# First weights behind the loads of nine units, their scaling queued behind the cast in front, and units 9 to 11 transposed on TensorE

## Chip, cores and metric

The kernel runs on one core of one Trainium2 chip. The metric is the time of one execution on the device, in microseconds (us). Lower is better. Three runs of the kernel before took 585.72, 586.73 and 589.5 us; the median is 586.73.

Engine names as in the profile: PE is TensorE's matmuls, PEld its loads of the stationary operand, DVE is VectorE, ACT is ScalarE, POOL is GpSimd, SP is the engine whose queue issues the transfers (DMAs).

## The reference

Gated linear attention over 4 batches, 8 heads, 768 tokens and a head width of 48, then a two-layer feed-forward network over all 3072 tokens.

```
for t in range(S):
    state = alpha[:, :, t, :, None] * state + np.einsum('bhd,bhe->bhde', k[:, :, t], v[:, :, t])
    y[:, :, t] = np.einsum('bhd,bhde->bhe', q[:, :, t], state)
...
x = np.ascontiguousarray(attn_out.transpose(0, 2, 1, 3)).reshape(B * S, H * D)
h = x @ w_in
g = np.maximum(0.01 * h, h)
out = (g @ w_out).astype(np.float32)
```

q, k, v and alpha are float32. The weights (384 x 2048 and 2048 x 384) are float64, and the kernel reads them as pairs of 32-bit words.

## The kernel before

**Units, blocks, items.** The attention is cut into 24 units: unit u is one chunk of 128 tokens of one batch, the four batches of a chunk one after another (units 0 to 3 have no state yet, line 317). Three units make a block of 384 tokens; there are 8 blocks. The feed-forward network works on a block and one of 16 slices f of 128 hidden columns: one such pair is an item (i, f). A first half (`ffn_in`, line 401) is nine matmuls of 128 x 384 into one of two `ph` banks, then ScalarE (lines 410, 413) and VectorE (411, 415) make the high part gh and the low part gl of the hidden values (three buffers each). A second half (`ffn_out`, line 420) is nine matmuls into the three banks of the block's sums; it is written two items later (LAG). `finish` (434) copies the sums with ScalarE and stores them.

**A unit, step by step.** `scans(u)` transposes alpha, then VectorE makes the running products forward (246) and their reversed counterpart (251). `scaled_q`, `scaled_k` transpose q and k and multiply (266, 274). `scores` are 16 matmuls (283), `mask_scores` copies and masks them, `k_tokens` turns k back, `outputs` makes y and from it x, a high part on ScalarE (342) and a low part on VectorE (343), and `next_state` updates the state. The generator `attention` yields between these steps and overlaps unit u + 1 with unit u. After each third unit, `gather` moves a few rows of x by DMA, and the block's items can start.

**Two ways to transpose** (line 212). Units under EARLY = 9 are loaded with one row per token (`load`, line 113) and transposed on TensorE into PSUM, four transposes per tensor (218). Later units are loaded in another layout by four transfers per tensor (121) and transposed on VectorE by one instruction per tensor (222). The same constant decides in `mask_scores` whether the second half of the scores is masked by ScalarE and GpSimd or by VectorE (291). alpha, q and k have two buffers each, v three; a load of unit u + 2 is written as soon as unit u has been transposed, that of v (`load_values`) for u + 3 in `outputs(u)`.

**Weights.** `load_weights(f)` issues five transfers on SP into one of four raw tiles. `convert(f)` turns float64 into a high and a low float32 part: ScalarE scales the upper words (line 200), VectorE works in six steps (201, 202, 204 to 207), and between them ScalarE casts the high part (203), which line 206 needs.

**PSUM.** Two banks are `ph`. Six belong to two kinds, "a" and "b", three each. At first the attention takes both kinds in turn; from line 457 on only "a", since block 0 keeps its sums in "b", block 1 in "a" and all later blocks in "b".

**What sets the order.** The program is a trace of instructions in the order of the Python code; the tile framework then orders each engine's queue with a timing model of its own (`schedule_with_timeline_sim=True`, line 623), earlier lines first where several are ready. Each engine then works its queue in that order and waits on semaphores. `behind(key)` (line 165) adds an edge: what is written within it, on the engine of the named instruction, is queued behind that instruction. In the kernel before, the attention of units 0 to 5 runs first (lines 446 to 452), with the weight loads of f = 0 to 3 written after its 18th, 26th, 34th and 42nd step. Conversions 0 to 2 stand behind the x of units 3 to 5 on VectorE. Then three items of block 0 are written with the rest of the attention of units 6 to 8 among them (8 steps per item), then three items of block 1, and from f = 3 on pairs: (0, f), (1, f), with the conversion of f + 2. From block 2 on, 1.5 steps of attention are written per item.

Of the kernel before, what the change touches and what calls it, by code (L numbers as in the profile page):

```python
# [9 lines left out]
F32 = mybir.dt.float32  # L10
# [12 lines left out]
def gated_linear_attn_ffn(ctx, tc, q, k, v, alpha, w_in, w_out, out):  # L23
    nc = tc.nc
# [8 lines left out]
    NF = DF // P  # L33
    UPB = 3
    HB = 64
    BR = HB + D
# [3 lines left out]
    NU = len(units)  # L40
# [13 lines left out]
    NBITS, NPW, NRAW = 1, 1, 4  # L54
    T4 = 4
    RUN = T4 * D
    PITCH = RUN + GAP
    EARLY = 3 * UPB
    FIRST = 3
    LAG = 2  # L60
    SL = 8 * UPB


# [34 lines left out]
    def w_out_of(f, n):  # L98
        return w_sb[f][:, n, DM:]

    def loaded(u, i):
        return loads_sb[i][u % len(loads_sb[i])]

# [3 lines left out]
    def load(u, i):  # L107
# [4 lines left out]
        t, src = loaded(u, i), (alpha, q, k)[i]  # L112
        if u < EARLY:
            n = H if u or i else H // 2
# [13 lines left out]
    def load_values(u):  # L128
        if u >= NU:
            return  # L130
        tb, b = units[u]
        nc.sync.dma_start(
            vals_sb[u % NV].rearrange("t (h d) -> t h d", h=H),
            v[b, :, tb * C:(tb + 1) * C, :].rearrange("h t d -> t h d"),
        )
# [24 lines left out]
    runs = [(0, D, 0, 1, 2 * D), (D, GAP, 6 * D, NG, 1), (HB, D, D, 1, 2 * D), (BR, GAP, 7 * D, NG, 1)]  # L160


    jobs, made = {}, {}

    def behind(*key):

        return tc.issue_after(made[key].ins) if key in made else nullcontext()

    def load_weights(f):
        if f >= NF:  # L170
# [11 lines left out]
    def convert(f):  # L182
        if f >= NF:
            return
        raw = jobs.pop(f)
        w_sb[f] = cst.tile([P, 2, 2 * DM], F32R, name=f"w{f}")
        hi, lo = w_sb[f][:, HIGH, :], w_sb[f][:, LOW, :]
        if not f64:
            val = raw[:, :, 0:P].bitcast(F32)
            hi, lo = (t.rearrange("p (g f) -> p g f", f=P) for t in (hi, lo))  # L190
            nc.scalar.copy(hi, val)
            nc.vector.tensor_tensor(lo, val, hi.bitcast(F32), ALU.subtract)
            return
        words = raw.rearrange("p g (f w) -> p (g f) w", w=2)
        top, low = words[:, :, 1], words[:, :, 0]
        bits = cvp.tile([P, 2 * DM], I32, name="bits", bufs=NBITS)
        pw = cvp.tile([P, 2 * DM], I32, name="pw", bufs=NPW)
        val, rest = bits.bitcast(F32), pw.bitcast(F32)

        nc.scalar.mul(top.bitcast(F32), top.bitcast(F32), 2.0 ** -112)  # L200
        nc.vector.tensor_scalar(bits, top, 3, 0x7FFFFFF8, ALU.logical_shift_left, ALU.bitwise_and)
        nc.vector.scalar_tensor_tensor(bits, top, -0x80000000, bits, ALU.bitwise_and, ALU.bitwise_or)
        nc.scalar.copy(hi, val)
        nc.vector.tensor_scalar(pw, bits, -0x800000, None, ALU.bitwise_and)
        nc.vector.scalar_tensor_tensor(rest, low.bitcast(U32), 2.0 ** -52, rest, ALU.mult, ALU.mult)
        nc.vector.tensor_tensor(val, val, hi.bitcast(F32), ALU.subtract)
        made["w", f] = nc.vector.tensor_tensor(lo, rest, val, ALU.add)

    def banks4():
        return bank().rearrange("r (p n) -> r p n", p=NP)  # L210

    def transposed(u, i, name, **kw):

        src = loaded(u, i)
        if u < EARLY:
            ps = banks4()
# [69 lines left out]
    def mask_scores(u):  # L286
        ss = live[u].pop()
        sm = [atp.tile([P, NP, C], F32, name="sm", bufs=3) for _ in (0, 1)]
        for s in (0, 1):
            if s and u >= EARLY:  # L290
                nc.vector.tensor_tensor(sm[s], ss[s], mask.unsqueeze(1).broadcast_to([P, NP, C]), ALU.mult)
                continue
            nc.scalar.copy(sm[s], ss[s])  # L293
            nc.gpsimd.affine_select(  # L294
                out=sm[s], in_=sm[s], compare_op=ALU.is_ge, fill=0.0, base=0, pattern=[[0, NP], [1, C]], channel_multiplier=-1
            )
        masked[u] = sm
# [11 lines left out]
    def outputs(u):  # L309
        tb, b = units[u]  # L310
        i, j = divmod(u, UPB)
        pe, qs, ktok = live[u][:3]
        V, W = vals_sb[u % NV], state[b]
        at = i % 3 * (NG + 1)
        y = banks4()

        if tb:
            for p in range(NP):
                nc.tensor.matmul(
                    y[0:BR, p, :], W[0:BR, p, :], qs[0:BR, p, :], start=p == 0, stop=False, skip_group_check=True  # L320
                )
        for p in range(NP):
            for s, lo, m in ((0, 0, D if tb else HB), (1, HB, D)):
                c = (2 * p + s) * D
                nc.tensor.matmul(  # L325
                    y[lo:lo + m, p, :], V[:, c:c + m], masked[u][s][:, p, :],
                    start=not tb and p == 0, stop=p == NP - 1, skip_group_check=True,
                )
        del masked[u]
        kv = None  # L330
        if tb < NC - 1:
            kv = bank()[:, 0:NP * D].rearrange("d (p e) -> d p e", p=NP)
            for p in range(NP):
                for s, lo in ((0, 0), (1, HB)):
                    h = 2 * p + s
                    nc.tensor.matmul(
                        kv[lo:lo + D, p, :], ktok[:, p, lo:lo + D], V[:, h * D:(h + 1) * D], start=True, stop=True
                    )
        load_values(u + NV)
        live[u] = pe, kv  # L340
        xh, xl = (x_sb[0:BR, at:at + NP, n, j * C:(j + 1) * C] for n in (0, 1))
        nc.scalar.copy(xh, y[0:BR])
        made["x", u] = nc.vector.tensor_tensor(xl, y[0:BR], xh.bitcast(F32), ALU.subtract)

    def next_state(u):
# [25 lines left out]
    ready = set()  # L371

    def attention(first, last):

        for u in range(first - 1, last):
            new, old = u + 1 < last, u >= first
            if new:
                scans(u + 1)
                yield
            if old:  # L380
                scores(u)
                yield
                mask_scores(u)
                yield
                k_tokens(u)
                yield
            if new:
                scaled_q(u + 1)
                yield
                scaled_k(u + 1)  # L390
                yield
            if old:
                outputs(u)
                yield
                next_state(u)
                if u % UPB == UPB - 1:
                    gather(u // UPB)
                    ready.add(u // UPB)
                yield
# [40 lines left out]
            nc.sync.dma_start(out[r:r + P, :], o)  # L440


    LOADS = 18, 26, 34, 42
    st = attention(0, EARLY)
    n = 0
    while 1 not in ready:
        next(st)
        n += 1
        if n == 3:
            load_values(NV - 1)  # L450
        if n in LOADS:
            load_weights(LOADS.index(n))
    for f in range(FIRST):
        with behind("x", UPB + f):
            convert(f)
    loaded_f = len(LOADS)
    kinds[:] = "a"


    items = [(0, f, None, SL / FIRST, "b") for f in range(FIRST)]  # L460
    items += [(1, f, f + FIRST if f < LAG else None, 0, "a") for f in range(FIRST)]
    for f in range(FIRST, NF):
        items += [(0, f, f + LAG, 0, "b"), (1, f, None, 0, "a")]
    items += [(i, f, None, SL / NF, "b") for i in range(2, NB) for f in range(NF)]

    gs = {}
    due, emitted, held = 0.0, 0, 0
    for n in range(len(items) + LAG):
        slices = 0
        if n < len(items):  # L470
            i, f, weights, slices, _ = items[n]
            if f == 0:
                if i == 1:
                    for _ in st:
                        pass
                if i == 2:
                    st, held = attention(EARLY, NU), 8
                while i not in ready:
                    next(st)
                emitted, due = 0, 0.0  # L480
            if loaded_f < NF:
                load_weights(loaded_f)
                loaded_f += 1
            if weights is not None:
                with behind("x", EARLY - 1):
                    convert(weights)
            gs[n] = ffn_in(i, f)
        for half in range(2):
            due += slices / 2
            while emitted < due:  # L490

                with behind(*(("w", NF - 1) if held else ())):
                    next(st, None)
                held = max(held - 1, 0)
                emitted += 1
            if half == 0 and n >= LAG:
                i, f, _, _, tag = items[n - LAG]
                ffn_out(i, f, gs.pop(n - LAG), tag)
# [129 lines left out]
```

## Time and profile before

| what | us |
|---|---|
| median of three runs | 586.73 |
| the profiled execution's own time | 587.34 |
| its span, first to last instruction | 585.6 |
| PE busy / PEld busy | 548.0 / 510.8 |
| DVE busy | 397.7 |
| ACT busy | 234.3 |
| POOL busy | 53.2 |
| ACT waiting at line 200 for a DMA of weights, 13 times | 28.4 |
| mean granted TensorE clock, share of full speed | 0.973 |

The span is 1.7 us shorter than the execution's own time. A row of the profile gives an engine, a line of the kernel, the operation, output and inputs, and a count; in order of time it begins with start and length in us, and brackets at its end give how long the engine was idle before it and what it waited for. Lengths of neighbouring rows overlap a little, since an instruction's end and the next one's start are not the same event: pitch from start to start is what an engine really spends. A stage row gives, for a stretch of time, the busy us of each engine, the clock that TensorE was granted, and what the DMA engines did. Stages here do not have one limit: the start, the pairs of blocks 0 and 1, and the long rest from about 216 us differ, and are read apart.

### The profile page before, as it was taken

What the parts mean: (1) busy time and instruction counts of PE and PEld (TensorE: products, weight loads), DVE (VectorE), ACT (ScalarE), POOL (GpSimd) and SP (SyncE); (2) the same over time, 40 slices, a digit from 0 to 9 for tenths busy, and PEclk for the clock granted to TensorE, in tenths of its full rate; (3) what the DMA queues carried; (4) which work ended last, traced back from release to release, by engine and by line L of the source; (5) the groups of instructions that cost most, each with busy time, mean ns of one, the idle gap of its engine ahead of it and who ended that gap; (6) DMA issues with size and microseconds to landing.
All of it is one profiled execution on the core that took longest, in us unless ns stands there. A gap on an engine that the chain in (4) does not pass through costs nothing. (4 is left out here: it accounts for less than half of the span.)

```text
span 585.6 us, 9944 instructions
## 1 busy us (share of the span) xinstructions
PE 548.0 (94%) x3742; PEld 510.8 (87%) x3742; DVE 397.7 (68%) x726; ACT 234.3 (40%) x486; POOL 53.2 (9%) x108
## 2 busy tenths in 40 slices
PE   6887899798989899999999989999999999999995
PEld 4766799687879888999899989998999999999994
DVE  6879854889889989688837775767848553333331
ACT  3553543454344364443533344344433243334332
POOL 4122112000000001011101101101001000000000
PEclk9899689899989999999999999999999999999998
DMA  9999953444320544224512342222311110001001
GB/s 162 192 194 169 175 129 84 120 109 108 109 54 1 120 135 104 61 63 97 141 26 64 73 120 45 64 50 65 99 25 39 35 42 0 1 21 42 0 1 45
DMA packets 92981, 46.62 MB, mean 80 GB/s; under 512 B 57856, under 2 KB 90112, under 8 KB 92928
## 3 DMA queue, kind: packets, MB, share of 16 engines
q1 hardware_dynamic: 92928, 45.93, 36.6%
q8 instruction: 31, 0.51, 0.4%
q14 instruction: 22, 0.18, 0.1%
HBM read 38.83 MB, written 4.72 MB: 74 GB/s over the span
## 5 line engine op out<-in xcount | busy, mean ns | idle before, releaser
L407 PE MATMUL ph<-large,w 128*128 128x384 f32 x1152 | 231.5, 345 | 13.5 <-DVE t L411 6.7
L407 PEld LDWEIGHTS ph<-large,w 128*128 128x128 f32 x1152 | 202.8, 191 | 22.5 <-DVE t L411 10.5
L428 PE MATMUL b<-w,gh 128*128 128x384 f32 x672 | 170.1, 344 | 0.9 <-ACT t L438 0.6
L411 DVE TENSOR_TENSOR t<-ph,t 128x384 f32<-128x384 f32 x128 | 70.1, 551 | 85.7 <-ACT t L410 85.2
L428 PEld LDWEIGHTS b<-w,gh 128*128 128x128 f32 x672 | 120.1, 190 | 5.3 <-ACT gh L413 1.9
L410 ACT ACTIVATE t<-ph 128x384 f32<-128x384 f32 x128 | 62.3, 489 | 144.8 <-PE ph L407 130.9
L428 PE MATMUL b<-w,gl 128*128 128x384 f32 x336 | 107.7, 340 | 1.6 <-DVE gl L415 1.6
L415 DVE TENSOR_TENSOR gl<-t,gh 128x384 fp32r<-128x384 f32 x128 | 70.8, 557 | 38.4 <-ACT gh L413 38.3
L413 ACT CAST gh<-t 128x384 fp32r<-128x384 f32 x128 | 65.4, 512 | 71.6 <-DVE t L411 69.6
L428 PEld LDWEIGHTS b<-w,gl 128*128 128x128 f32 x336 | 62.4, 189 | 3.2 <-DVE gl L415 2.6
L283 PE MATMUL a<-qs,ks 48*128 48x128 f32 x336 | 37.9, 295 | 2.7 <-DVE qs L266 1.7
L283 PEld LDWEIGHTS a<-qs,ks 48*128 48x128 f32 x336 | 31.2, 195 | 10.3 <-issue 5.9
L358 POOL TENSOR_TENSOR small<-us,pe 48x192 f32<-48x192 f32 x32 | 18.5, 577 | 175.1 <-DVE us L357 173.8
L294 POOL TENSOR_SCALAR_AFFINE_SELECT sm<-sm 128x512 f32<-128x512 f32 x33 | 22.0, 672 | 134.7 <-ACT sm L293 134.3
L257 ACT ACTIVATE e<-pc 128x512 f32<-128x512 f32 x24 | 15.2, 632 | 31.9 <-DVE rc L251 17.9
L200 ACT ACTIVATE raw<-raw 128x768 f32<-128x768 f32 x16 | 14.6, 916 | 28.4 <-DMA raw<-in_moe_w_in_dram 28.4
L246 DVE TENSOR_TENSOR_SCAN pc<-e,small 128x128 f32<-128x128 f32 x60 | 22.0, 422 | 0.5
L325 PE MATMUL a<-sm,small 128*48 128x128 f32 x288 | 22.2, 279 | 0.0
L428 PE MATMUL a<-w,gh 128*128 128x384 f32 x96 | 21.7, 349 | 0.0
L222 DVE STREAM_TRANSPOSE ks<-small 128x512 f32<-128x512 f32 x15 | 16.6, 1104 | 6.9 <-PE a L304 6.9
L258 POOL COPY pe<-pc 128x4 f32<-128x4 f32 x24 | 7.9, 328 | 144.7 <-DVE pc L246 144.2
L222 DVE STREAM_TRANSPOSE e<-small 128x512 f32<-128x512 f32 x15 | 16.6, 1104 | 6.0 <-ACT e L257 5.8
(77 smaller groups left out, 537.2 us busy)
## 6 DMA issues: line engine op xcount, KB each, us to landing
raw<-in_moe_w_out_dram SPq DMA_DIRECT2D x16, 384.0 KB, 3.7
small<-in_v_dram SPq DMA_DIRECT2D x24, 192.0 KB, 4.1
raw<-in_moe_w_in_dram SPq DMA_DIRECT2D x32, 144.0 KB, 4.0
out_dram<-t SPq DMA_DIRECT2D x24, 192.0 KB, 2.1
small<-in_alpha_dram SPq DMA_DIRECT2D x32, 96.0 KB, 2.2
small<-in_q_dram SPq DMA_DIRECT2D x30, 96.0 KB, 2.4
small<-in_k_dram SPq DMA_DIRECT2D x30, 96.0 KB, 2.2
small<-in_alpha_dram SPq DMA_DIRECT2D x30, 80.0 KB, 2.3
```

Of the source, the lines that this page charges most:

```text
L222: nc.vector.transpose(t.rearrange("r p (j t) -> r p t j", t=T4), src.rearrange("r p (t d) -> r p t d", t=T4)[:, :, :, 0:32],)
L246: nc.vector.tensor_tensor_scan(pc[:, p, :], aT[:, p, :], ones.broadcast_to([P, C]), 1.0, ALU.mult, ALU.mult)
L283: nc.tensor.matmul(ss[s][:, p, :], ks[lo:lo + D, p, :], qs[lo:lo + D, p, :], start=True, stop=True)
L294: nc.gpsimd.affine_select(out=sm[s], in_=sm[s], compare_op=ALU.is_ge, fill=0.0, base=0, pattern=[[0, NP], [1, C]], channel_multiplier=-1)
L325: nc.tensor.matmul(y[lo:lo + m, p, :], V[:, c:c + m], masked[u][s][:, p, :], start=not tb and p == 0, stop=p == NP - 1, skip_group_check=True,
L358: nc.gpsimd.tensor_tensor(W[r, :, r], us[r], pe[r].broadcast_to([D, NP, D]), ALU.mult)
L407: nc.tensor.matmul(ph, w_in_of(f, wn, g), xt[:, g, :], start=n == 0, stop=n == 3 * NG - 1)
L410: nc.scalar.mul(t, ph, 0.01)
L411: nc.vector.tensor_tensor(t, ph, t, ALU.max)
L413: nc.scalar.copy(gh, t)
L415: nc.vector.tensor_tensor(gl, t, gh.bitcast(F32), ALU.subtract)
L428: nc.tensor.matmul(po[j], gt[:, js], w_out_of(f, wn), start=f == 0 and n == 0, stop=f == NF - 1 and n == 2)
```

## The change

1. The constant EARLY, which decides on load layout and transposes, goes from 9 to 12 units. A new constant AHEAD = 9 takes over its other roles: how many units are written ahead, and which units mask half of their scores on VectorE.
2. The attention of all nine units is written first, with no items among it. The load of f = 0 is queued on SP behind the load of v of unit 6, f = 1 behind that of unit 7, f = 2 and f = 3 behind that of unit 8.
3. Conversions 0 to 2 are queued on VectorE behind `ks` (line 274) of units 6, 7 and 8. Later conversions stay behind the x of unit 8.
4. The scaling of line 200 is queued on ScalarE behind the cast of line 203 of the f in front; for f = 0 behind the x of unit 5 on ScalarE (line 342).
5. The items of blocks 0 and 1 are pairs from f = 0 on, each with the conversion of f + 3.

```diff
-    EARLY = 3 * UPB
-    FIRST = 3
+    EARLY = 4 * UPB
+    AHEAD = 3 * UPB
     LAG = 2
+    SOON = 3
...
-        nc.sync.dma_start(
+        made["v", u] = nc.sync.dma_start(
             vals_sb[u % NV].rearrange("t (h d) -> t h d", h=H),
...
-        nc.scalar.mul(top.bitcast(F32), top.bitcast(F32), 2.0 ** -112)
+        with behind("hi", f - 1) if f else behind("xh", AHEAD - SOON - 1):
+            nc.scalar.mul(top.bitcast(F32), top.bitcast(F32), 2.0 ** -112)
...
-        nc.scalar.copy(hi, val)
+        made["hi", f] = nc.scalar.copy(hi, val)
...
-            if s and u >= EARLY:
+            if s and u >= AHEAD:
                 nc.vector.tensor_tensor(sm[s], ss[s], mask.unsqueeze(1).broadcast_to([P, NP, C]), ALU.mult)
...
-        nc.scalar.copy(xh, y[0:BR])
+        made["xh", u] = nc.scalar.copy(xh, y[0:BR])
...
-    LOADS = 18, 26, 34, 42
-    st = attention(0, EARLY)
-    n = 0
-    while 1 not in ready:
-        next(st)
-        n += 1
-        if n == 3:
+    st = attention(0, AHEAD)
+    loaded_f = 0
+    for n, _ in enumerate(st):
+        if n == 2:
             load_values(NV - 1)
-        if n in LOADS:
-            load_weights(LOADS.index(n))
-    for f in range(FIRST):
-        with behind("x", UPB + f):
+        u = AHEAD - SOON + min(loaded_f, SOON - 1)
+        if loaded_f < NRAW and ("v", u) in made:
+            with behind("v", u):
+                load_weights(loaded_f)
+            loaded_f += 1
+    for f in range(SOON):
+        with behind("ks", AHEAD - SOON + f):
             convert(f)
-    loaded_f = len(LOADS)
     kinds[:] = "a"


-    items = [(0, f, None, SL / FIRST, "b") for f in range(FIRST)]
-    items += [(1, f, f + FIRST if f < LAG else None, 0, "a") for f in range(FIRST)]
-    for f in range(FIRST, NF):
-        items += [(0, f, f + LAG, 0, "b"), (1, f, None, 0, "a")]
+    items = []
+    for f in range(NF):
+        items += [(0, f, f + SOON, 0, "b"), (1, f, None, 0, "a")]
     items += [(i, f, None, SL / NF, "b") for i in range(2, NB) for f in range(NF)]
...
-                if i == 1:
-                    for _ in st:
-                        pass
                 if i == 2:
-                    st, held = attention(EARLY, NU), 8
+                    st, held = attention(AHEAD, NU), 8
...
             if weights is not None:
-                with behind("x", EARLY - 1):
+                with behind("x", AHEAD - 1):
                     convert(weights)
```

More of the change, by code (lines that the diff above doesn't have):

```diff
@@ L99, in w_out_of, with behind @@
         return w_sb[f][:, n, DM:]
+    made = {}
+    def behind(*key):
+        return tc.issue_after(made[key].ins) if key in made else nullcontext()
     def loaded(u, i):
@@ L160, in gated_linear_attn_ffn @@
     runs = [(0, D, 0, 1, 2 * D), (D, GAP, 6 * D, NG, 1), (HB, D, D, 1, 2 * D), (BR, GAP, 7 * D, NG, 1)]
-    jobs, made = {}, {}
-    def behind(*key):
-        return tc.issue_after(made[key].ins) if key in made else nullcontext()
+    jobs = {}
     def load_weights(f):
```

## The prediction, made before the changed kernel had run

> **What bounds the kernel now.** I read the busy time by stage first, then DVE's and PE's rows in order of time, SP's queue, and the waits of single stages. Columns of the stage view: stage and length, then busy us of PE, PE's weight loads, DVE, ACT and POOL, the granted clock, the DMA share and GB/s.
>
> ```profile
> 0.00:24.00 24.00, 18.50 (x164) 14.65 (x164) 17.60 (x47) 10.48 (x22) 8.16 (x27) 1.00 1.15 173
> 24.00:63.00 39.00, 31.24 (x279) 26.36 (x278) 31.71 (x63) 19.94 (x41) 9.16 (x16) 0.86 1.14 185
> 63.00:103.00 40.00, 37.73 (x284) 33.57 (x283) 25.11 (x50) 15.88 (x33) 7.93 (x15) 0.88 0.58 123
> 103.00:168.00 65.00, 56.09 (x285) 51.16 (x285) 57.21 (x86) 28.57 (x51) 0.00 (x0) 0.95 0.42 111
> 168.00:193.00 25.00, 24.59 (x135) 23.23 (x135) 23.30 (x36) 10.04 (x19) 0.00 (x0) 0.99 0.00 1
> 193.00:216.00 23.00, 20.09 (x112) 18.44 (x111) 22.06 (x46) 9.40 (x23) 0.56 (x3) 1.00 0.54 137
> 240.00:570.00 330.00, 327.38 (x2281) 313.76 (x2280) 196.37 (x358) 124.32 (x263) 24.50 (x44) 1.00 0.22 52
> ```
>
> From 240 on PE is busy 327.4 of 330 us: nothing in this change makes that stretch shorter, and PE work added to it lengthens it. What can be won lies ahead of about 216. There three things bound in turn. Up to 63 us the DMA engines are full (share 1.14). From 63 to 103 PE is busy 37.7 of 40, at a clock of 0.88, on attention units 7 and 8 mixed with six feed-forward items. From 103 to 193 DVE leads with 80.5 of 90 us.
>
> How the first stage holds up the units shows in the first scan of each unit on DVE (units 1, 2, 3, 4, 7 and 8), and in the x of units 1 and 8:
>
> ```profile
> 9.97 1.36 DVE L246 TENSOR_TENSOR_SCAN pc<-b,small 128x128 f32<-128x128 f32 x4
> 15.99 1.36 DVE L246 TENSOR_TENSOR_SCAN pc<-b,small 128x128 f32<-128x128 f32 x4 [0.43 <-PE b L218]
> 22.47 1.37 DVE L246 TENSOR_TENSOR_SCAN pc<-b,small 128x128 f32<-128x128 f32 x4
> 23.75 0.67 DVE L343 TENSOR_TENSOR large<-b,large 112x512 fp32r<-112x512 f32 x1
> 33.99 1.37 DVE L246 TENSOR_TENSOR_SCAN pc<-b,small 128x128 f32<-128x128 f32 x4 [0.36 <-PE b L218]
> 63.29 1.36 DVE L246 TENSOR_TENSOR_SCAN pc<-a,small 128x128 f32<-128x128 f32 x4
> 80.58 1.37 DVE L246 TENSOR_TENSOR_SCAN pc<-a,small 128x128 f32<-128x128 f32 x4
> 100.04 0.69 DVE L343 TENSOR_TENSOR large<-a,large 112x512 fp32r<-112x512 f32 x1 [2.24 <-ACT large L342]
> ```
>
> Units 1 to 3 follow each other by 6.0 and 6.5 us, 6.25 on average. Then the pitch is 11.5 (unit 3 to 4), and 17.3 from unit 7 to 8. The first break is the weights':
>
> ```profile
> 17.33 2.50 SPq L176 DMA_DIRECT2D raw<-in_moe_w_in_dram  x4
> 20.41 0.67 SPq L116 DMA_DIRECT2D small<-in_k_dram  x1
> 26.13 1.09 PE L218 MATMUL a<-small 128*128 128x128 f32 x4 [2.01 <-DMA small<-in_k_dram]
> ```
>
> Unit 3's k is issued behind four transfers of weights that are converted much later, and PE waits for it. The four transposes then take 1.09 us, against 0.60 in a row further below, so the clock fell as well.
>
> **Part 1, first weights behind the loads of nine units.** Now f = 0, 1, 2 and 3 go behind the v of units 6, 7, 8 and 8; each is five transfers on SP. Taken away are four weight tiles of five transfers from the queue ahead of units 3 to 6. The 12 feed-forward halves of f = 0..2 are no longer written between units 6 to 8, but all 32 items come behind unit 8. Unit loads themselves need little: at pitch 6.25 a unit's four 192 KB tensors are 126 GB/s, under the 173 to 185 that the queue moves.
>
> So the units should keep 6.25: unit 8's scan at 22.47 + 5 x 6.25 = 53.7, and its x 13.8 later (unit 1: 9.97 to 23.75), at 67.5, if conversions 0 to 2 cost nothing. What one costs:
>
> ```profile
> 114.05 0.55 DVE L201 TENSOR_SCALAR bits<-raw 128x768 int32<-128x768 int32 x1
> 117.97 1.01 DVE L411 TENSOR_TENSOR t<-ph,t 128x384 f32<-128x384 f32 x2
> 118.91 0.95 DVE L207 TENSOR_TENSOR w<-pw,bits 128x768 fp32r<-128x768 f32 x1
> 119.77 1.02 DVE L415 TENSOR_TENSOR gl<-t,gh 128x384 fp32r<-128x384 f32 x2
> 120.71 0.55 DVE L201 TENSOR_SCALAR bits<-raw 128x768 int32<-128x768 int32 x1
> 187.51 0.55 DVE L201 TENSOR_SCALAR bits<-raw 128x768 int32<-128x768 int32 x1
> ```
>
> From 114.05 to 120.71 DVE has no pause: 6.66 us are one conversion and the two items of a pair. The items take 0.94 (117.97 to 118.91) and 0.94 (119.77 to 120.71), so a conversion 4.8. Three are 14.4; they stand behind the k of units 6, 7 and 8. Unit 8 has no successor whose 6.25 us of scans would fill its tail; this and about 1 us of gaps take 7.3. The rest, 7, I add: attention and three conversions end at 74.5. Bounds: 67.5 (all hidden) and 82 (none). This is an estimate; DVE is the engine that it rests on.
>
> Three pairs at DVE's 6.66 bring the first matmul of item (0, 3) to 94.5. Before it stands here, and (0, 15), behind the last conversion, in the second row:
>
> ```profile
> 105.87 3.98 PE L407 MATMUL ph<-large,w 128*128 128x384 f32 x14 [1.80 <-DVE w L207]
> 192.04 0.62 PE L407 MATMUL ph<-large,w 128*128 128x384 f32 x2
> 242.95 1.72 PE L407 MATMUL ph<-large,w 128*128 128x384 f32 x9
> 244.51 0.52 PE L428 MATMUL b<-w,gh 128*128 128x384 f32 x2
> ```
>
> The start so gains 11.4. Nine matmuls take 1.56 us on PE (242.95 to 244.51), an item 3.12, a pair 6.24. PE has idle places in the attention, and two ph banks and three gh let up to three first halves, 4.7 us, run there; I count half: 14 in all. Bounds: 82 + 3 x 7.35 (mean pitch of conversions now, 114.05 to 187.51 over ten) = 104, a gain of 1.8; and 67.5 + 3 x 6.24 - 4.7 = 81.5, a gain of 24.
>
> **Part 2, scaling behind the cast in front.** From (0, 3) to (0, 15) are 12 pairs in 86.2 us, 7.18 each. The waits of 105 to 166 (us, times, longest), and one case of how they follow each other:
>
> ```profile
> ACT raw L200 <- DMA raw<-in_moe_w_in_dram: 18.2, 8, 3.2
> DVE bits L206 <- ACT w L203: 3.5, 4, 1.2
> DVE t L411 <- ACT t L410: 3.5, 3, 1.7
> ...
> 160.83 0.92 ACT L200 ACTIVATE raw<-raw 128x768 f32<-128x768 f32 x1 [3.19 <-DMA raw<-in_moe_w_in_dram]
> 161.65 0.81 ACT L203 CAST w<-bits 128x768 fp32r<-128x768 f32 x1
> 162.50 0.96 DVE L206 TENSOR_TENSOR bits<-bits,w 128x768 f32<-128x768 f32 x1 [1.07 <-ACT w L203]
> 163.98 1.08 PE L407 MATMUL ph<-large,w 128*128 128x384 f32 x4 [2.02 <-DVE t L411]
> ```
>
> ACT stands 3.2 us at the scaling L200 of weights that are needed three conversions later. The cast L203 of the current f is queued behind it, DVE's L206 waits for that cast, and PE for DVE. With the new order edge L200 of f comes behind L203 of f - 1, when its weights have long landed, so ACT doesn't stop. Late next would be L201, if L200 started late; between L203's end and the next L201 DVE has L206 and then the 2.74 us from 117.97 to 120.71, which hide the 0.92 of L200; without that cover it costs 0.92 a conversion. Gain: at most the 7.0 us that DVE waited on ACT, at least nothing; after the last L200 (168 to 193) DVE still idles 1.7 in 25 us, so I take 4.
>
> **Part 3, units 9 to 11 on TensorE.** DVE loses nine stream transposes; PE gets 36 transposes in nine groups of four; loads become one transfer instead of four per tensor.
>
> ```profile
> L222 DVE STREAM_TRANSPOSE e<-small 128x512 f32<-128x512 f32 x15 | 16.6, 1104 | 6.0 <-ACT e L257 5.8
> 86.02 0.60 PE L218 MATMUL a<-small 128*128 128x128 f32 x4
> 86.38 1.83 PE L407 MATMUL ph<-large,w 128*128 128x384 f32 x9
> 206.49 0.68 PE L428 MATMUL a<-w,gl 128*128 128x384 f32 x3
> 215.87 0.48 ACT L438 COPY t<-a 128x384 f32<-128x384 f32 x1 [1.60 <-PE a L283]
> ```
>
> A group holds PE 0.36 us (86.02 to 86.38): 3.3 in a stretch where PE sets the end; bound 9 x 0.60 = 5.4. DVE's 9.9 us are worth at most PE's idle 2.9 of 193 to 216; I take 1.5. New is a wait: these tiles need an "a" bank, and block 1's sums hold all three until ACT has copied them, the last at 215.87. I take 2 us for it, bounds 0 and the 9.4 from 206.49 to 215.87.
>
> **Sum.** 14 + 4 - 3.3 + 1.5 - 2 = 14.2 us less. The profiled execution took 587.3 (span 585.6 and 1.7 around it), 0.6 over the median; so 573.1 in its terms, **572.5** as a median. With the start's gain, the largest term, between 6 and 22 and the rest (0.2 together) as they are, that is 565 to 581; all bounds at once would be 556 and 600.
>
> **The clock.** Granted clock in the first stages is 1.00, 0.86 and 0.88; the PE gap of 2.0 us ahead of 26.13 was enough to halve the rate of the transposes. [...]
>
> **Rivals.**
>
> - *The start only moves.* Conversions fit nowhere (82), pairs stay at 7.35, the waits on ACT return as waits on DVE: 1.8 + 0 - 3.3 - 2, about 3 us lost, 590; with half of the start's gain 585. For it: DVE is near full from 103 on. Against: DVE was busy only 74.4 of 103 us before.
> - *The clock falls in the attention alone* (slower). Without feed-forward items PE has many short gaps; if each lowers the rate as at 26.13, units keep the 11.5 pitch of unit 3 to 4: scan of unit 8 at 22.5 + 5 x 11.5 = 80, x at 94, with 7 of conversions 101, (0, 3) at 121, 15 lost: 587.3 + 15 - 4 + 3.8 = 602. It decides from a pitch of about 9. Against: units 1 to 3 ran alone at 6.25.
> - *Banks stop PE at units 9 to 11* (slower). The transposes stand in PE's queue ahead of block 2's matmuls: 9.4 for the copies, and 2 us (the wait ahead of 26.13) for each of nine groups until a scan frees a bank, 27 in all, less the 2 counted: 598. It decides from 16 us of waits at L218. Against: units 6 to 8 already live with three "a" banks, in a stretch where PE is busy 37.7 of 40.
> - *All holes are used.* Start gain 24, waits 7, less 3.3: 560.
>
> **How the numbers follow.** Forecast (565 to 581) 0.62; all holes used 0.15; the start only moves 0.15; clock 0.04; banks 0.04. A measurement of this kernel tells about 1% from no change, 581 and 593. Faster by over 1%: 0.62 + 0.15, 0.77; slower 0.04 + 0.04, 0.08; the third, 0.15, is within. The range 561 to 584 leaves about 0.2 out.
>
> **What would show it.** Right: scan of unit 8 at 54 to 58; x of unit 8 near 75; (0, 3) at 90 to 96; (0, 15) at 170 to 178; no DMA wait at L200 behind 100; 144 transposes at L218 and 12 stream transposes of each tile. Wrong: pitch over 8 us in units 3 to 6; DVE waiting for raw weights at L201; PE waiting over 10 us at L218 behind 170; or (0, 15) earlier by 15 us and the end not, which would mean that the later stretch has grown.

## The result, and the profile after

| | us |
|---|---|
| before, median of four runs in this comparison | 586.23 |
| changed kernel, median of four runs (565.25 to 570.1) | 566.33 |
| ratio, with its 95% interval | 0.9663 [0.9604, 0.9722] |
| profiled execution of the changed kernel: own time, span | 565.25, 563.1 |
| mean granted TensorE clock (before: 0.973) | 0.987 |

The changed kernel is faster by 3.4%, some 20 us. In the two profiled executions the difference is 587.34 - 565.25 = 22.1 us.

The stage view of the changed kernel from 63 us on, with the columns and the borders of the one of before:

```profile
63.00:103.00 40.00, 38.56 (x266) 35.76 (x267) 38.01 (x60) 19.96 (x36) 6.99 (x8) 0.96 0.83 162
103.00:168.00 65.00, 64.22 (x357) 61.04 (x356) 63.88 (x99) 33.06 (x57) 0.00 (x0) 1.00 0.32 85
168.00:193.00 25.00, 24.00 (x139) 22.88 (x138) 12.17 (x26) 10.63 (x23) 0.19 (x1) 1.00 0.26 70
```

From 63 to 103 DVE does 38.0 us of work where it did 25.1. From 103 to 168 it does 63.9 where it did 57.2; PE's busy time there rises from 56.1 to 64.2, and the clock from 0.95 to 1.00. In the last row DVE has only 12.2 us to do, where it had 23.3: the pairs of blocks 0 and 1 are over by then.

Matmul groups date the stages. In the kernel before, the first four matmuls for f = 3 (two each of (0, 3) and (1, 3), which need only the high part of the weights), and two groups of six second-half matmuls of one form:

```profile
103.11 0.96 PE L407 MATMUL ph<-large,w 128*128 128x384 f32 x4
164.90 2.06 PE L428 MATMUL b<-w,gh 128*128 128x384 f32 x6
186.30 1.23 PE L428 MATMUL b<-w,gh 128*128 128x384 f32 x6
```

And in the changed kernel, in order of time: outputs of units 3 and 4 (34.79 to 45.81), early first halves (59.24, 64.34), outputs of unit 7 (65.96), the first matmuls for f = 3 with the rest behind them, those for f = 15, and the start of block 3:

```profile
34.79 0.43 PE L329 MATMUL b<-sm,small 128*64 128x128 f32 x2 [1.72 <-POOL sm L298]
36.87 1.86 PE L329 MATMUL b<-sm,small 128*48 128x128 f32 x14
45.81 1.07 PE L329 MATMUL b<-sm,small 128*48 128x128 f32 x14
59.24 0.61 PE L411 MATMUL ph<-large,w 128*128 128x384 f32 x2
64.34 0.98 PE L411 MATMUL ph<-large,w 128*128 128x384 f32 x2 [2.42 <-DMA large<-large]
65.96 1.90 PE L323 MATMUL b<-qs,small 112*112 112x128 f32 x8
89.46 1.08 PE L411 MATMUL ph<-large,w 128*128 128x384 f32 x4
92.49 2.24 PE L411 MATMUL ph<-large,w 128*128 128x384 f32 x12
169.07 1.08 PE L411 MATMUL ph<-large,w 128*128 128x384 f32 x4 [0.25 <-DVE t L415]
253.44 3.36 PE L411 MATMUL ph<-large,w 128*128 128x384 f32 x18 [2.36 <-DMA large<-large]
259.26 1.83 PE L411 MATMUL ph<-large,w 128*128 128x384 f32 x9 [1.19 <-DVE t L415]
```

With them the 22.1 us come apart:

| stretch | before | after | gained |
|---|---|---|---|
| start to the first matmuls of (0, 3) | 103.11 | 89.46 | 13.65 |
| (0, 3) to (0, 15), twelve pairs | 103.11 to 192.04: 88.9 | 89.46 to 169.07: 79.6 | 9.3 |
| (0, 15) to the last instruction | 192.04 to 585.6: 393.6 | 169.07 to 563.1: 394.0 | -0.5 |
| around the span | 1.74 | 2.15 | -0.4 |

The third row shows that nothing won early was given back, and nothing more was won. The first scan of units 1, 5, 6 and 8 on DVE, the x of unit 8, the end of conversion 2, and the first step of conversions 4 and 15:

```profile
10.10 1.36 DVE L250 TENSOR_TENSOR_SCAN pc<-b,small 128x128 f32<-128x128 f32 x4
...
35.90 1.37 DVE L250 TENSOR_TENSOR_SCAN pc<-b,small 128x128 f32<-128x128 f32 x4 [1.38 <-PE b L222]
44.85 1.37 DVE L250 TENSOR_TENSOR_SCAN pc<-b,small 128x128 f32<-128x128 f32 x4 [1.16 <-PE b L222]
...
58.68 1.36 DVE L250 TENSOR_TENSOR_SCAN pc<-b,small 128x128 f32<-128x128 f32 x4
79.26 0.69 DVE L347 TENSOR_TENSOR large<-a,large 112x512 fp32r<-112x512 f32 x1
83.13 0.95 DVE L211 TENSOR_TENSOR w<-pw,bits 128x768 fp32r<-128x768 f32 x1
91.58 0.56 DVE L205 TENSOR_SCALAR bits<-raw 128x768 int32<-128x768 int32 x1
164.54 0.56 DVE L205 TENSOR_SCALAR bits<-raw 128x768 int32<-128x768 int32 x1
```

Units 1 to 8 follow each other by (58.68 - 10.10) / 7 = 6.94 us. Conversions follow each other by (164.54 - 91.58) / 11 = 6.63, where they followed by 7.35.

### The profile page after: what moved, and what is told of

Read it like the earlier page. It is cut to its first block, busy times and chain, and to the rows that moved or that the text cites. A ratio compares the mean times of both kernels' runs of the same rounds, so it can differ in the third digit from the quotient of the medians.

```text
span 563.1 us, 9996 instructions
## 1 busy us (share of the span) xinstructions
PE 536.4 (95%) x3778; PEld 504.2 (90%) x3778; DVE 387.5 (69%) x717; ACT 234.1 (42%) x486; POOL 55.3 (10%) x108
## 4 chain that ended last, share of the span: by engine, by line
PE 72%; DVE 15%; DMA 6%; issue 3%; ACT 2%; SPq 1%; POOL 0%; DVEq 0%; ACTq 0%
PE ph L411 30%; PE b L432 27%; PE a L287 3%; DMA large<-large 3%; PE a L329 2%; PE a L323 2%; PE a L432 2%; DVE t L415 2%; DVE pc L250 2%; DVE rc L255 2%; DVE bits L210 1%; DVE pw L209 1%; DMA out_dram<-t 1%; PE b L222 1%; PE a L308 1%
## 5 line engine op out<-in xcount | busy, mean ns | idle before, releaser
L411 PE MATMUL ph<-large,w 128*128 128x384 f32 x1152 | 227.8, 340 | 9.0 <-DMA large<-large 6.5
L411 PEld LDWEIGHTS ph<-large,w 128*128 128x128 f32 x1152 | 199.2, 188 | 16.8 <-DVE t L415 6.6
L298 POOL TENSOR_SCALAR_AFFINE_SELECT sm<-sm 128x512 f32<-128x512 f32 x33 | 24.2, 745 | 132.7 <-ACT sm L297 132.5
L287 PE MATMUL a<-qs,ks 48*128 48x128 f32 x312 | 32.6, 292 | 1.0 <-DVE ks L278 1.0
L287 PEld LDWEIGHTS a<-qs,ks 48*128 48x128 f32 x312 | 26.7, 192 | 6.7 <-issue 4.5
L207 ACT CAST w<-bits 128x768 fp32r<-128x768 f32 x16 | 13.4, 839 | 23.9 <-DVE bits L206 23.9
L261 ACT ACTIVATE e<-rc 128x512 f32<-128x512 f32 x24 | 15.1, 631 | 17.1 <-DVE rc L255 16.8
L329 PE MATMUL a<-sm,small 128*48 128x128 f32 x256 | 20.0, 279 | 0.1
L250 DVE TENSOR_TENSOR_SCAN pc<-e,small 128x128 f32<-128x128 f32 x48 | 18.6, 440 | 0.5
L226 DVE STREAM_TRANSPOSE e<-small 128x512 f32<-128x512 f32 x12 | 13.3, 1106 | 6.8 <-ACT e L261 6.6
```

The lines of the kernel that those rows point to most:

```text
L250: nc.vector.tensor_tensor_scan(pc[:, p, :], aT[:, p, :], ones.broadcast_to([P, C]), 1.0, ALU.mult, ALU.mult)
L261: nc.scalar.activation(junk, t, AF.Abs, accum_out=acc[:, 2 * u + n:2 * u + n + 1])
L287: nc.tensor.matmul(ss[s][:, p, :], ks[lo:lo + D, p, :], qs[lo:lo + D, p, :], start=True, stop=True)
L298: nc.gpsimd.affine_select(out=sm[s], in_=sm[s], compare_op=ALU.is_ge, fill=0.0, base=0, pattern=[[0, NP], [1, C]], channel_multiplier=-1)
L329: nc.tensor.matmul(y[lo:lo + m, p, :], V[:, c:c + m], masked[u][s][:, p, :], start=not tb and p == 0, stop=p == NP - 1, skip_group_check=True,
L411: nc.tensor.matmul(ph, w_in_of(f, wn, g), xt[:, g, :], start=n == 0, stop=n == 3 * NG - 1)
```

## The experiments

All ratios are to the kernel before, timed on the same chip in the same series. Each of the change's three main edits was taken out of the changed kernel and put alone into the kernel before; after these come two edits together, and two attempts on what the trace after still shows.

**The changed kernel without the scaling edge.**

```diff
-        with behind("hi", f - 1) if f else behind("xh", AHEAD - SOON - 1):
-            nc.scalar.mul(top.bitcast(F32), top.bitcast(F32), 2.0 ** -112)
+        nc.scalar.mul(top.bitcast(F32), top.bitcast(F32), 2.0 ** -112)
```

> The changed kernel without the order edge at the scaling of the weights. Theory (edges carry the gain in the pairs): ScalarE stands again some 2 us for each f at the scaling, waiting for weights, and a pair of items goes from 6.63 back towards 7.2 to 7.4 us; 12 pairs make it 7 to 9 us slower than the changed kernel, about 574. Rival (the longer lead does it: each conversion is now written three f ahead instead of two): pairs stay at 6.6 to 6.7 and the time within 2 us of the changed kernel, 565 to 568.

Measured: 573.96 us, ratio 0.9821 [0.9763, 0.9880]. ACT's longest wait from 103 to 168 (us, times, longest), the stage row of that stretch, and the first step of conversions 4 and 15:

```profile
ACT raw L203 <- DMA raw<-in_moe_w_in_dram: 17.0, 7, 3.1
```
```profile
103.00:168.00 65.00, 59.13 (x319) 54.27 (x318) 57.71 (x90) 28.67 (x52) 0.00 (x0) 1.00 0.32 86
```
```profile
90.75 0.55 DVE L204 TENSOR_SCALAR bits<-raw 128x768 int32<-128x768 int32 x1
171.79 0.55 DVE L204 TENSOR_SCALAR bits<-raw 128x768 int32<-128x768 int32 x1
```

ACT's stops for weights are back, seven of them, up to 3.1 us long. The pitch is 81.04 / 11 = 7.37, that of the kernel before. The changed kernel's longer lead (conversion of f + 3 instead of f + 2) is still in this one and helps nothing here: it is the edge that frees the pairs, worth (7.37 - 6.63) x 11 = 8.1 us over these conversions. The granted clock is 1.00 here, so the slow pairs of the kernel before don't come from their clock of 0.95: at full clock DVE idles as much (57.7 busy of 65, before 57.2).

**The scaling edge alone in the kernel before.**

```diff
-        nc.scalar.mul(top.bitcast(F32), top.bitcast(F32), 2.0 ** -112)
+        with behind("hi", f - 1):
+            nc.scalar.mul(top.bitcast(F32), top.bitcast(F32), 2.0 ** -112)
...
-        nc.scalar.copy(hi, val)
+        made["hi", f] = nc.scalar.copy(hi, val)
```

> The kernel before with nothing but the order edge: the scaling of f behind the cast of f - 1. Theory (the edge is what shortens the pairs): ScalarE's wait for weights behind 105 us goes, 12 pairs lose about 0.5 to 0.7 us each, 6 to 9 us in all: 577 to 581. Rival (it needs the longer lead): 584 to 588.

Measured: 578.08 us, ratio 0.9879 [0.9822, 0.9935], by the ratio 7.1 us. The first step of two conversions ten pitches apart, and the stage row of the late pairs:

```profile
112.64 0.55 DVE L202 TENSOR_SCALAR bits<-raw 128x768 int32<-128x768 int32 x1
178.98 0.55 DVE L202 TENSOR_SCALAR bits<-raw 128x768 int32<-128x768 int32 x1
```
```profile
168.00:193.00 25.00, 23.15 (x127) 21.47 (x126) 24.76 (x41) 10.23 (x20) 0.19 (x1) 1.00 0.19 47
```

66.34 / 10 = 6.63: without any other part of the change, the pitch falls to that of the changed kernel. Taken out or put in, the edge shows the same two pitches. It needs neither the longer lead nor the new start. DVE's idle time from 168 to 193, 1.7 us before, is 0.24 here: it went with the waits ahead of it.

**The first loads' place alone in the kernel before** (with the definitions of `made` and `behind` moved up, and the load of v recorded).

```diff
-            load_weights(LOADS.index(n))
+            f = LOADS.index(n)
+            with behind("v", 4 + f):
+                load_weights(f)
```

> The kernel before with nothing but its first four weight loads queued behind the v of units 4, 5, 6 and 7; items and steps are written as before. Theory (the place of the loads makes the start shorter): units 3 to 5 no longer wait for their loads, their pitch is 6 to 7 us, and the time falls by 4 to 10 us: 576 to 582. Rival (items among units 6 to 8, not the loads, hold up the start): units 3 to 5 are earlier, but PE-bound units 7 and 8 end at 98 to 101 us as before, 584 to 588.

Measured: 577.3 us (574.64 to 581.49), ratio 0.9897 [0.9829, 0.9965], by the ratio 6.0. The first scan of unit 4, and the x of unit 8:

```profile
27.43 1.37 DVE L247 TENSOR_TENSOR_SCAN pc<-b,small 128x128 f32<-128x128 f32 x4
89.21 0.69 DVE L344 TENSOR_TENSOR large<-a,large 112x512 fp32r<-112x512 f32 x1
```

Unit 4's scan comes at 27.4 instead of 34.0, unit 8's x at 89.2 instead of 100.0. The transfers queued ahead of the units' k were therefore a cause of the late start, as read from SP's queue. By the medians the end moves by about half of that; in the profiled executions (574.64, the fastest of its four, against 587.34) it moves by 12.7 us, more than all of it. How much of the earlier unit 8 reaches the end is so not settled.

**The changed kernel with the first loads not held back.**

```diff
-            with behind("v", u):
-                load_weights(loaded_f)
+            load_weights(loaded_f)
```

> The changed kernel, whose first four weight loads are written at the same place but not queued behind the v of units 6 to 8. Theory (the place of the loads in SP's queue makes the start shorter): the loads move forward among those of units 3 to 6, the pitch of these units goes from 7 us to 8 or more, and the start gives back 5 to 10 us: 571 to 577. Rival (the start is shorter because all nine units run without items among them): no more than 2 us slower, 565 to 568.

Measured: 570.46 us (566.9 to 572.54), ratio 0.9754 [0.9681, 0.9827]. The first and the last of the loads on SP, then the x of unit 8:

```profile
13.39 1.10 SPq L182 DMA_DIRECT2D raw<-in_moe_w_out_dram  x1
...
35.80 2.15 SPq L179 DMA_DIRECT2D raw<-in_moe_w_in_dram  x4
```
```profile
86.55 0.69 DVE L347 TENSOR_TENSOR large<-a,large 112x512 fp32r<-112x512 f32 x1
```

Without the edge to v the framework pulls the loads forward to 13.4 to 35.8, and unit 8's x is 7.3 us late. The median is some 4 us above the changed kernel's, a little below what was expected, and the interval is 1.5% wide, wider than the difference. So the traces show what the edge does to the units; how much of it reaches the end, this pair settles only roughly.

**Units 9 to 11: the changed kernel with them on VectorE, and the kernel before with them on TensorE.** The first has one line changed; the second has the new constants and AHEAD in four places.

```diff
-    EARLY = 4 * UPB
+    EARLY = 3 * UPB
```

> The changed kernel with units 9 to 11 transposed on VectorE again. Theory (this part is about even: PE gains 3.3 us of transposes, VectorE loses 9 us in the stretch where block 2 starts): within 3 us of the changed kernel, 564 to 569. Rival (the part is a loss, since PE sets the end there): 3 to 5 us faster, 561 to 563. Second rival (the part carries gain, since VectorE at the start of block 2 holds up PE): 570 or more.

```diff
-    EARLY = 3 * UPB
+    EARLY = 4 * UPB
+    AHEAD = 3 * UPB
```

> The kernel before with nothing but units 9 to 11 loaded by token and transposed on TensorE. Theory (about even): 584 to 589. Rival (VectorE is what block 2 waits for): 578 to 583. Rival (banks stop PE): over 592.

Measured: 565.86 us, ratio 0.9681 [0.9623, 0.9739], and 583.07 us, ratio 0.9989 [0.9964, 1.0015]. Taken out or put in, the part makes no difference that can be measured. Groups of the changed kernel's line 222:

```profile
L226 DVE STREAM_TRANSPOSE e<-small 128x512 f32<-128x512 f32 x12 | 13.3, 1106 | 6.8 <-ACT e L261 6.6
L222 PE MATMUL a<-small 128*128 128x128 f32 x76 | 13.5, 306 | 4.5 <-POOL small L161 3.3 <-DMA small<-in_alpha_dram 0.5 <-ACT t L442 0.5
L222 PE MATMUL b<-small 128*128 128x128 f32 x68 | 13.4, 331 | 1.6 <-DVE rc L255 0.9 <-DMA small<-in_q_dram 0.6
```

76 + 68 = 144 transposes on PE and 12 per tile on DVE are what the change says. PE's wait for ScalarE to copy block 1's sums (line 442) is there, but 0.5 us.

**Scaling edge and loads' place together in the kernel before.** Both edits above.

> The kernel before with the loads queued behind v of units 4 to 7 and with the scaling edge, but its own order of items and units and conversions written two f ahead. Theory (two independent gains, in stages that follow each other): 6.5 + 5.7 add up, 571 to 573; the 5 to 6 us left to the changed kernel belong to the order of units and items. Rival (both remove the same wait for weights): no more than 2 us below the better of the two alone, 575 to 578. Second rival (these two are all of it): 565 to 568.

Measured: 570.85 us (567.5 to 573.6), ratio 0.9728 [0.9698, 0.9758]. In the same series the changed kernel gave:

> The changed kernel again, on the same chip as the three that follow: 564 to 568. Theory and rival agree; it is the measure for the others.

567.28 us, ratio 0.9691 [0.9667, 0.9714]. By the ratio the two edits bring 15.9 us; alone they brought 7.1 and 6.0, 13.1 together. Within their intervals (each is some 3 to 4 us wide to either side) they add up.

What is left for all the rest (the nine units written without items, the pairs from f = 0 on, the lead of three, units 9 to 11) is 0.9728 - 0.9691, 2.2 us. The two intervals overlap, so whether that is anything stays open.

**The changed kernel with more steps of attention per item in block 2.** PE waits 2.4 us for the gather of block 3's rows at 253.44; this writes the attention of units 9 to 11 and so the gather earlier.

```diff
-    items += [(i, f, None, SL / NF, "b") for i in range(2, NB) for f in range(NF)]
+    items += [(i, f, None, (SL + 4 * (i == 2)) / NF, "b") for i in range(2, NB) for f in range(NF)]
```

> The changed kernel with 1.75 instead of 1.5 attention steps written per item of block 2. Theory (block 3 starts 2.4 and 1.2 us late since x of unit 11 and its gather come late): unit 11 is ready earlier, both waits go, 2 to 4 us faster than the changed kernel, 562 to 565. Rival (PE has the same work to do and the wait moves elsewhere): within 1 us, 565 to 568.

Measured: 566.94 us, ratio 0.9668 [0.9645, 0.9692]: the changed kernel's time. The gather in the changed kernel, then here the gather and PE's first matmuls behind it:

```profile
249.03 1.22 SPq L371 DMA_DIRECT2D large<-large  x2
```
```profile
245.92 1.21 SPq L371 DMA_DIRECT2D large<-large  x2
250.76 3.22 PE L411 MATMUL ph<-large,w 128*128 128x384 f32 x9 [3.51 <-DMA large<-large]
```

The gather is issued 3.1 us earlier, PE arrives earlier as well and waits 3.5 instead of 2.4. More steps written do not take the wait away; they move it.

**The changed kernel with two of the first loads behind the gather of block 1.** f = 2 and f = 3 leave SP's queue ahead of that gather.

```diff
-            nc.sync.dma_start(
+            made["g", i] = nc.sync.dma_start(
...
-        if loaded_f < NRAW and ("v", u) in made:
-            with behind("v", u):
+        key = ("v", u) if loaded_f < 2 else ("g", 1)
+        if loaded_f < NRAW and key in made:
+            with behind(*key):
```

> The changed kernel with the loads of f = 2 and 3 queued behind the gather of block 1 instead of behind v of unit 8. Theory (the gather is issued 2 us late, behind weights, and PE and unit 8's transposes wait for it): the wait of 2.4 us ahead of item (1, 0) shrinks, unit 8 is some 2 us earlier, and the time falls by 1 to 3 us, 563 to 566. Rival (VectorE sets the pace there, and conversion 2 comes later instead): within 1 us, 565 to 568.

Measured: 564.03 us (561.52 to 566.72), ratio 0.9634 [0.9606, 0.9662], against 0.9691 for the changed kernel in the same series: about 3.3 us less, and the fastest kernel here, with intervals that just miss each other. The gather in the changed kernel, then gather, first matmuls of (1, 0) and the x of unit 8 in this one:

```profile
57.65 1.20 SPq L371 DMA_DIRECT2D large<-large  x2
```
```profile
55.54 1.23 SPq L371 DMA_DIRECT2D large<-large  x2
...
61.55 0.60 PE L411 MATMUL ph<-large,w 128*128 128x384 f32 x2
...
76.21 0.69 DVE L347 TENSOR_TENSOR large<-a,large 112x512 fp32r<-112x512 f32 x1
```

The 2.42 us that PE waited for the gather at 64.34 (4.13 in the repeated run of the changed kernel) are gone, and two of the matmuls take 0.60 us at 61.55, where in the changed kernel they took 0.98 at 64.34, at a granted clock of 0.50. Unit 8's x is 3.05 us earlier, which is the size of the gain at the end.

## Why the prediction came out as it did

The profiled execution of the changed kernel came 7.9 us below the 573.1 of the sum (565.25). Part by part:

**The start: 14 predicted, 13.65 measured.** The mechanism is shown: SP's queue held up the units, and the loads' place alone brought unit 8's x from 100.0 to 89.2. But the sum within this term is right through two errors that cancel.

- Attention and conversions 0 to 2 ended at 83.13 + 0.95 = 84.1, not at 74.5. Units follow by 6.94, not 6.25, which is 4.8 us over seven units. The largest break is 8.95 us between units 5 and 6 (35.90 to 44.85): just ahead of it, at 34.79, PE has waited 1.72 us for a mask of unit 3, and at 36.87 fourteen matmuls take 1.86 us that take 1.07 one unit later (45.81); the granted clock is 0.50 from 37.0 to 43.75 and 1.00 from 44 on. That is the rival "the clock falls in the attention alone", come true for those 6.75 us; its pitch of 9 was met once, not on average. The sum had no term for the clock; from 24 to 63 the granted clock is 0.91 on average, where it was 0.86. Unit 8's x also came 20.6 us behind its scan, not 13.8, because first halves of items and conversions run between them.
- What ran there was missing behind it. I let three pairs cost 20 us behind the conversions, less 2.35 for early first halves. First halves ran from 59.24 on, and from the end of conversion 2 to (0, 3) only 89.46 - 84.08 = 5.4 us passed. I also took the row at 105.87 as the first matmul of (0, 3); two of its matmuls and two of (1, 3) stand at 103.11, and counted so the gain is 13.65, counted from row to rest (105.87 to 92.49) 13.4.

**The scaling edge: 4 predicted, 9.3 measured in the twelve pairs; this is the step that failed.** The mechanism held at both experiments: pitch 7.37 without the edge, 6.63 with it, in either kernel. The waits of the changed kernel from 103 to 168:

```profile
ACT w L207 <- DVE bits L206: 17.2, 7, 2.8
```

The view has no row of a DMA at the scaling line any more. ACT still stands idle for about as long (17.2, against 18.2 at line 200 before), but now it waits for DVE, which sets the pace (busy 63.9 of 65 us): idle time that costs nothing there. The size was wrong at its upper bound. I took the 7.0 us that DVE was seen to wait on ACT in 105 to 166 as the most that could come back, and halved it because of idle time seen from 168 to 193. The bound should have been all of DVE's idle time in the pairs, (65 - 57.21) + (25 - 23.30) = 9.5 us, against 9.3 measured. (The 9.3 hangs on the rows that one counts between; eleven conversions of the changed kernel with and without the edge differ by 8.1. The time of the edge alone, 7.1 us with an interval of 3.8 to 10.4, would by itself not exclude 4; the pitch does.) My own row of 6.66 us for a conversion and a pair without a pause gave nearly the same: twelve pairs of 7.41 - 6.66 are 9.0, though with the 7.18 that I used, which leaves out the matmuls at 103.11, only 6.2. The idle time of the late part, which I took for something that stays, went with the edge alone (24.76 of 25 busy). PE's lower rate behind such waits (2.06 us for six matmuls at 164.90, at a granted clock of 0.50 from 165.0 to 168.25; 1.23 at 186.30, at 1.00) was not what cost the time: without the edge, but at a clock of 1.00, the pitch is the same 7.37.

**Units 9 to 11: -3.8 predicted in all, no difference measured.** The two single experiments say even, and the stretch from (0, 15) on differs by 0.5 us. What PE waited for in that stretch, before:

```profile
PE ph L407 <- DVE e L222: 1.8, 1, 1.8
...
PE ph L407 <- DMA large<-large: 0.8, 1, 0.8
PE b L428 <- DVE gl L415: 0.8, 1, 0.8
PE b L428 <- ACT t L438: 0.6, 1, 0.6
```

then the first row of the same view in the changed kernel, three of the four rows (from 164 on) in the changed kernel with these units on VectorE, and the first row in the kernel before with them on TensorE:

```profile
PE ph L411 <- DMA large<-large: 4.0, 3, 2.4
```
```profile
PE b L432 <- ACT t L442: 1.8, 1, 1.8
PE ph L411 <- DMA large<-large: 1.7, 2, 0.9
...
PE a L432 <- DVE gl L419: 1.0, 1, 1.0
```
```profile
PE ph L408 <- DMA large<-large: 3.3, 3, 1.9
```

Around the start of block 2, PE waits less with the units on TensorE. In the kernel before four waits for gl, t and ScalarE's copies of sums stand from 198.47 to 211.86 (0.75, 0.88, 0.58 and 0.71, together 2.9 us); the changed kernel has 1.0 us in three waits from 169.07 to 190.57, and 4.0 us in four with the units back on VectorE (176.09 to 191.28); the kernel before with them on TensorE has none there. So the relief of DVE, put at 1.5, was there and was some 2 to 3 us. The wait for the copies of block 1's sums, put at 2, is 0.5. The 1.8 us under `DVE e L222` have no part in this: they stand at 339.74, ahead of block 4, whose transposes run on VectorE in all these kernels.

The loss stands at the start of block 3. PE waits there for the gather and, one item on, for t: 2.36 and 1.19 us in the changed kernel (253.44, 259.26), 1.88 and 0.98 in the kernel before with the units on TensorE (269.89, 275.50). With the units on VectorE block 3 starts without such a wait, in the kernel before (275.74) as in the changed one (256.71). So about as much waiting came at block 3's start as went at block 2's, and no step of the prediction had it. These are single executions, and why the gather comes late there was not found; writing it earlier did not get the time back. The 3.3 us of PE's time for 36 more transposes don't show in the end; PE's busy time over the stretch grew by 0.5 (380.8 to 381.3):

```profile
192.04:585.60 393.56, 380.82 (x2605) 362.57 (x2604) 243.71 (x450) 149.88 (x324) 27.93 (x52) 0.99 0.24 59
```
```profile
169.07:563.10 394.03, 381.35 (x2640) 365.09 (x2640) 234.73 (x441) 149.28 (x323) 28.06 (x52) 1.00 0.23 57
```

DVE's is 9.0 less, as counted. Why PE's busy time grew so little was not taken apart. The rival "banks stop PE" fell.

The 7.9 us are so made up of the edge (5.3 too little), units 9 to 11 (3.3 too much loss), and the start and the time around the span (0.7 the other way). The measured 566.33 lies in the range of 565 to 581, but that range was opened for the start alone, which came as forecast by two errors that cancel; that it still covers a miss in the terms that it held fixed is luck. Two of the signs named for "right" were missed by a little: the scan of unit 8 came at 58.68 (54 to 58) and its x at 79.26 (near 75). "All holes are used", 560, was the rival nearest in kind, but only the pairs came out like it: DVE is busy 63.9 of 65 us there, and the start kept its holes.

## What to carry to other kernels

When an engine stops for something that is needed only later, and needed work stands behind the stop (ACT here, seven stops and 17.0 us from 103 to 168 without the edge), price the stop by up to all idle time of the engine that paces the stage, and not only by the waits that are named after it: later idle time can be its after-effect, as it was here (DVE's 1.7 us from 168 to 193, 0.24 with the edge alone). Edges in such queues are then worth trying one by one: the scaling behind a cast, and weights' loads behind what the next units need, brought 7 and 6 us alone and 16 together, while shifting work from one engine to another (units 9 to 11) brought nothing. A transfer that is written early can stand ahead of the urgent one that comes behind it: with two loads moved behind a gather, the gather was issued at 55.54 us instead of 57.65, and the whole was some 3 us shorter.

## What the runs showed of the hardware

Behind the first 10 us the profiles of the kernel before and of the changed kernel have eleven PE waits of 1.65 to 2.42 us. At seven of them PE's rate fell to about half, with a granted clock of 0.50 for 3 to 7 us: among them 1.72 us at 34.79 (1.86 us for fourteen matmuls, else 1.07; 0.50 from 37.0 to 43.75), 2.42 us at 64.34 (1.90 us for eight matmuls, else 1.13; 0.50 from 64.5 to 67.5; two matmuls of a first half took 0.98 where the kernel without the wait shows 0.60), and in the kernel before 2.02 us at 163.98 (2.06, else 1.23; 0.50 from 165.0 to 168.25). At four it did not, and the longest of these is 2.36 us, at 253.44: eighteen matmuls follow in 3.36 us, at a granted clock of 1.00. At the same place the kernel with two loads behind the gather waits less and is slower:

```profile
250.88 4.94 PE L411 MATMUL ph<-large,w 128*128 128x384 f32 x18 [1.93 <-DMA large<-large]
```

So between 1.65 and 2.42 us the length of the single wait does not decide in these profiles. What decides instead, no run here tells apart.

ScalarE kept the order of its queue wherever the theory needed it. In the kernel before, eight scalings from 109.26 to 160.83 waited 1.06 to 3.19 us each for their weights (18.2 us in all), and a cast ran right behind each of them, 0.8 to 1.2 us after its start. In the changed kernel without the edge there are seven such waits from 103 to 168, 17.0 us in all.
